# Weight rounding moved from the attention phase to the mixing phase, and couplings interleaved with another step

## The chip, the cores and the metric

One core of one Trainium2 chip runs the whole program. The metric is device microseconds of one execution; the figure before is the median of three runs. PE is TensorE, DVE VectorE, ACT ScalarE, POOL GpSimd, SP SyncE, which only issues DMAs here.

## What is computed

Three layers over 4 batches of 768 tokens and 384 features. The first is a recurrent attention with a delta rule (8 heads of 48), shown here as the reference has it; the second a gated unit with mixing over tokens; the third a channel mix.

```python
for t in range(S):
    y[:, :, t] = einsum('bhd,bhde->bhe', q[:, :, t], state)
    v_old = einsum('bhde,bhd->bhe', state, kt)
    state = state + bt * einsum('bhd,bhe->bhde', kt, vt - v_old)
...
h = gelu(x @ w_in); u, v = halves(h); v_n = layernorm(v) * g_ln
x = x + (u * (einsum('ts,bsd->btd', w_sg, v_n) + b_sg)) @ w_out
...
k = relu(xk @ w_k); out = sigmoid(xr @ w_r) * (k * k @ w_v)
```

xk and xr are blends of x with x one token earlier.

## The kernel before, in words

**Attention phase (to about 326 us).** Tokens are cut into 12 blocks of 64 (s = 0 to 11); two blocks make a group g (0 to 5); the 32 pairs of batch and head of a block are worked in two octets o = 0, 1 of 8 rows of 2. For each group, `gram` (L321) makes products of keys on PE, `solver` (L359) inverts the 32x32 diagonal blocks on DVE, many small instructions that end in a transpose to DT (L456), and `couple(g, k)` (L465) makes, for each half k = 0, 1 of the group, the off-diagonal block: 32 PE matmuls (L472; 64 records each, since a fp32 matmul appears twice) and two ACT copies back into GL (L475). For each s and o five steps follow: `st_rq` (L494: products with the state, residual r on DVE), `st_d` (L533: 32 matmuls of 32x32 with DT, then an ACT copy u1), `st_n` (L544: matmuls of GL with u1), `st_s` (L558: state) and `st_y` (L573: outputs, DMA into xT by `store_x`, L595).

The order on PE, ACT, DVE and POOL is the order of emission (a manual schedule). `slots` (L818) gives four slots per s; slot 0 is n(s-1, 1) and rq(s, 0), slot 1 d(s, 0), s(s-1, 1) and y(s-1, 1), slot 2 n(s, 0) and rq(s, 1), slot 3 d(s, 1), s(s, 0) and y(s, 0). `run` (L871) emits a slot's steps in three rounds (matmuls, first copies, rest), then `fill` and three calls of `tick` (L851). A call of `tick` is one point; 24 points are a group.

`fill` (L715) puts matmuls of the second layer's input projection between: v units (L651) of weight 1 and u units (L703) of weight 0.5; a v unit waits until 6 weight jobs are done, a u unit until 12. How many is planned: for points 24 to 95 from PACE, INST and COST (L880), otherwise from a slot time (SLOT, SLOT0) less the costs in `used` (L895). Where there are none, `keep_warm` (L737) runs idle matmuls.

`background` (L744), called in `tick` with a budget of 1.62 us of DVE, takes instructions from three kinds of streams by SHARE: layer-norm steps, the solver, weight jobs. It first runs what is due in `later`: a coupling goes there, two points after the solver's end, aligned to six points, the second half six points on (L459); scale_v four points after a y step (L593).

**Weight jobs.** The matrices w_in, w_out, w_k, w_r, w_v are of 64-bit numbers and are rounded to a high and a low part. `narrow` (L155) does one piece: a load on SP (L161), an ACT scaling (L165), four DVE instructions (L170, L172, L174, L176), a POOL add (L178) and then, `lag` points later, `split` (L118): an ACT copy to the high part and a POOL subtraction to the low part. `scratch` (L194) adds a store to DRAM by SP (L203). In the attention phase run 12 jobs of w_in (lag 0), 8 of w_out and 12 of w_k (128x256 each), in that order; two at a time early, later started every EVERY = 6 points while fewer than RUN run, from point 100 on every second point. `reload` (L209) and L1131 bring the rounded parts back.

**Mixing phase (326 to about 490 us).** Eight halves (b, t). `mix` (L1062) does four steps d of 18 matmuls (L976), with DVE (L1072, L1074, L1078) and ACT (L1075) after each; `project` (L1086) is the output projection of a half, 3 x 12 matmuls (L152) and one DVE add each (L1094). Beside them `side` (L1028) emits DVE instructions of weight jobs, here 3 of w_r and 8 of w_v: SD = 2 at each step d, one at each part of `project`. `turns` counts steps d; at most NRAW = 3 jobs are open. u and v come by SP (L1059, L244). After the seventh half POOL issues the reload of w_k (L1131), after the eighth that of w_v (L1142).

**Last phase.** Blends, `w_k`, `w_v` and `w_r` products (L152) and the output.

## Time and profile before

| | us |
|---|---|
| median of 3 runs | 741.13 (737.92 to 743.28) |
| the profiled execution | 737.01 |
| its span, first to last instruction | 735.2 |
| PE busy | 682.0 (93%) |
| DVE busy | 502.0 (68%) |
| ACT busy | 364.3 (50%) |
| POOL busy | 202.6 (28%) |
| mean granted TensorE clock | 0.972 of full speed |

The page gives one execution. A line such as L152 can be a helper's, so groups are told apart by their tiles. "Issue" in the chain is time in which an engine waited for nothing that the profile shows. In the chain and the waits, the name after an arrow is the instruction that ended last before the waiting one could start. Names of tiles such as sw0l or sg are slots that several tiles share in turn.

### The profile page before, as it was taken

How to read it: one execution, taken by the hardware profiler on the slowest of the kernel's cores; microseconds unless marked ns; L12 is line 12 of the kernel's file. 1: busy time of each engine (PE TensorE's matmuls, PEld its weight loads, DVE VectorE, ACT ScalarE, POOL GpSimd, SP SyncE). 2: the span in 40 equal slices, each digit the busy share in tenths (PEclk: the TensorE clock that was granted, in tenths of full speed). 3: DMA queues.
4: the chain of work that ended last, by engine and by line, in shares of the span. 5: the costliest groups of instructions: out<-in, count | busy, mean ns of one | idle time of the engine just before them, and what ended most of it. 6: DMA issues, size and time to landing. Idle time of an engine off the chain costs nothing.

```text
span 735.2 us, 24465 instructions
## 1 busy us (share of the span) xinstructions
PE 682.0 (93%) x10669; PEld 618.3 (84%) x10669; DVE 502.0 (68%) x992; ACT 364.3 (50%) x696; POOL 202.6 (28%) x257
## 2 busy tenths in 40 slices
PE   2568889999997998899999999999999999999998
PEld 2436668878886897789999999998989898999997
DVE  5999989978979695723558676798655564736251
ACT  2235676777765766864322323156444453525140
POOL 4033543454444555643041615330000000000000
PEclk8678999999998999999999999999999999999999
DMA  8402654665665458548853444367000000000000
GB/s 246 108 30 72 158 141 121 177 177 178 155 200 179 126 178 219 186 132 232 284 185 132 153 148 150 109 200 186 33 12 23 22 21 22 18 27 11 33 12 32
DMA packets 80938, 88.71 MB, mean 121 GB/s; under 512 B 24704, under 2 KB 63616, under 8 KB 80832
## 3 DMA queue, kind: packets, MB, share of 16 engines
q1 hardware_dynamic: 75520, 77.33, 35.6%
q0 software_dynamic: 5312, 9.83, 5.0%
q8 instruction: 83, 1.36, 0.8%
q14 instruction: 23, 0.19, 0.1%
HBM read 56.60 MB, written 25.82 MB: 112 GB/s over the span
## 4 chain that ended last, share of the span: by engine, by line
PE 78%; DVE 10%; issue 4%; ACT 4%; DMA 2%; POOL 1%; SPq 1%; ACTq 0%; POOLq 0%; DVEq 0%
PE ms L152 34%; PE ms L976 12%; PE ms L703 7%; PE ms L651 6%; PE ms L579 3%; PE rk L537 2%; PE rk L550 2%; PE rk L514 2%; PE sps L565 2%; PE ms L742 2%; PE ms L334 2%; DVE sg L356 2%; PE ms L472 2%; PE qk L517 1%; DVE sg L396 1%
## 5 line engine op out<-in xcount | busy, mean ns | idle before, releaser
L152 PE MATMUL ms<-wvh,sl 128*128 128x384 f32 x192 | 64.7, 337 | 0.5 <-DVE sl L124 0.5
L152 PE MATMUL ms<-wvh,sh 128*128 128x384 f32 x192 | 64.6, 337 | 0.1
L152 PE MATMUL ms<-wvl,sh 128*128 128x384 f32 x192 | 64.5, 336 | 0.0
L178 POOL TENSOR_TENSOR na<-na,raw 128x256 int32<-128x256 int32 (+2 forms) x43 | 38.7, 899 | 93.3 <-ACT gh L1075 40.7
L1075 ACT ACTIVATE gh<-w 128x384 fp32r<-128x384 f32 x32 | 16.8, 526 | 93.7 <-DVE w L1074 93.7
L152 PE MATMUL ms<-xm_hi,sw0h 128*128 128x512 f32 x144 | 56.1, 390 | 0.0
L152 PE MATMUL ms<-xm_hi,sw0l 128*128 128x512 f32 x144 | 56.1, 389 | 0.0
L152 PE MATMUL ms<-xm_lo,sw0h 128*128 128x512 f32 x144 | 56.0, 389 | 0.0
L124 DVE TENSOR_TENSOR sl<-sg,sh 128x512 fp32r<-128x512 f32 x48 | 33.2, 691 | 28.8 <-ACT sh L121 28.6
L976 PE MATMUL ms<-sw0h,g 128*128 128x384 f32 x192 | 50.2, 335 | 0.0
L976 PE MATMUL ms<-ws1h,g 128*128 128x384 f32 x192 | 49.9, 334 | 0.0
L121 ACT ACTIVATE sh<-sg 128x512 fp32r<-128x512 f32 x48 | 30.3, 631 | 33.9 <-DVE sg L1188 33.9
L1205 DVE TENSOR_TENSOR sg<-sg,ms 128x384 f32<-128x384 f32 x24 | 13.3, 552 | 49.4 <-PE ms L152 49.4
L356 DVE TENSOR_TENSOR sg<-sg,Yt 128x512 f32<-128x512 f32 (+4 forms) x72 | 43.3, 611 | 1.3
L530 POOL TENSOR_SCALAR_AFFINE_SELECT SQ<-SQ 64x512 f32<-64x512 f32 x36 | 28.2, 783 | 48.6 <-ACT SQ L529 47.5
L1187 ACT ACTIVATE sg<-ms 128x512 f32<-128x512 f32 x48 | 28.6, 596 | 26.1 <-PE ms L152 24.1
L1188 DVE TENSOR_TENSOR sg<-sg 128x512 f32<-128x512 f32 x48 | 33.2, 691 | 10.9 <-ACT sg L1187 10.8
L334 PEld LDWEIGHTS ms<-kT 64*32 64x32 f32 x640 | 18.5, 124 | 22.4 <-issue 14.5
L703 PE MATMUL ms<-xl,wiu_hi 128*128 128x256 f32 x144 | 37.0, 296 | 0.0
L152 PEld LDWEIGHTS ms<-wvh,sl 128*128 128x128 f32 x192 | 36.1, 188 | 0.8 <-DVE sl L124 0.8
L703 PE MATMUL ms<-xh,wiu_lo 128*128 128x256 f32 x144 | 36.4, 291 | 0.0
L152 PEld LDWEIGHTS ms<-wvh,sh 128*128 128x128 f32 x192 | 36.1, 188 | 0.4 <-ACT sh L121 0.4
(244 smaller groups left out, 2151.0 us busy)
## 6 DMA issues: line engine op xcount, KB each, us to landing
u_d<-ug SPq DMA_DIRECT2D x24, 256.0 KB, 4.0
u<-u_d SPq DMA_DIRECT2D x16, 384.0 KB, 4.1
vn_d<-v SPq DMA_DIRECT2D x22, 256.0 KB, 3.5
vk<-in_vk_dram SPq DMA_DIRECT2D x24, 192.0 KB, 4.0
vk<-in_vk_dram SPq DMA_DIRECT2D x12, 384.0 KB, 3.7
st<-vn_d SPq DMA_DIRECT2D x18, 256.0 KB, 3.1
out_dram<-sg SPq DMA_DIRECT2D x24, 192.0 KB, 1.9
kT<-in_kt_d_dram SPq DMA_DIRECT2D x8, 512.0 KB, 5.3
```

Of the source, the lines that this page charges most:

```text
L121: A.activation(hi, src, AF.Copy)
L124: eng_lo.tensor_tensor(lo, src, hi.bitcast(F32), op=ALU.subtract)
L152: T.matmul(pt, lhsT=a, rhs=b, start=(i == 0), stop=(i == n - 1))
L178: G.tensor_tensor(a.bitcast(I32), a.bitcast(I32), w_lo.bitcast(I32), op=ALU.add)
L334: T.matmul(gps[r:r + 32, p, c0:c1], lhsT=t[r:r + 64, u, 0:32], rhs=t[r:r + 64, u, c0:c1], start=True, stop=True)
L356: V.tensor_tensor(tv, vw(a_t, a_off, a_dims), vw(b_t, b_off, b_dims), op=ALU.mult)
L530: G.affine_select(out=pt, in_=pt, pattern=[[0, 8], [1, C]], compare_op=ALU.is_gt, fill=0.0, base=0, channel_multiplier=-1)
L651: T.matmul(vstat[g, b], lhsT=a[:, c], rhs=w[:, c], start=first, stop=last)
L703: T.matmul(vstat["u"][:, 2 * P * d:2 * P * d + 2 * P], lhsT=w[:, c, ds_], rhs=a[:, c].rearrange("p b t -> p (b t)"), start=first, stop=last)
L976: T.matmul(pt[:, :DM], lhsT=v[:, ds_], rhs=w, start=(c == 0 and i == 0), stop=(c == 5 and i == 2))
L1187: A.activation(r, pt, AF.Relu)
L1188: V.tensor_tensor(r, r, r, op=ALU.mult)
```

## The change

- The 12 jobs of w_k leave the attention phase and stand in the mixing phase, in a queue of their own ahead of those of w_r and w_v; each queue has three jobs open. `side` emits one DVE instruction at each step d and five at each part of `project`, and `turns` advances in `project` too.
- In a job the POOL add, the ACT copy and the POOL subtraction are apart: one, two and one points later in the attention phase; in the mixing phase only the copy is a turn later.
- `couple` gives its matmuls and its copies apart. The even d steps d(2g, 0) and d(2g, 1) emit, after each four of their matmuls, four of the coupling's half o; the copies follow in the third round.
- Jobs start every 12 points; three run at once also early; one w_in job more is started at the start; scale_v comes six points after y.
- PACE 0.0157 to 0.0152, SLOT 5.315 to 5.1, PAIR and AHEAD in the plan of `fill`.

```diff
-SV = 60
-RUN = (3, 2, 3)
+RUN = (3, 3, 3)
-EVERY = 6
+EVERY = 12
+NMIX = 12
-JLAG = 2
-SLOT = 5.315
+SLOT = 5.1
-LAGC = 2
-PACE = 0.0157
+PACE = 0.0152
+PAIR = 0.45
+AHEAD = 4.0
-SD = 2
+SD = (1, 5)
...
-        G.tensor_tensor(a.bitcast(I32), a.bitcast(I32), w_lo.bitcast(I32), op=ALU.add)
+        yield hops[0], lambda: G.tensor_tensor(a.bitcast(I32), a.bitcast(I32), w_lo.bitcast(I32), op=ALU.add)
...
-        yield lag, lambda: split(A, G, af, hi, lo)
+        yield 1 + hops[0], lambda: A.activation(hi, af, AF.Copy)
+        yield hops[0], lambda: G.tensor_tensor(lo, af, hi.bitcast(F32), op=ALU.subtract)
...
-    jobs += j1
+    jobs += j1[:-NMIX]
+    wk_jobs = j1[-NMIX:]
     n_rest = len(jobs)
+    hops = [1]
...
-            if g:
-                p = point[0] + LAGC
-                p += -p % 6 if p % 6 > 2 else 0
-                for k in range(2):
-                    later.append((p + 6 * k, lambda k=k: couple(g, k)))
...
             DT, u0, t = DTs[s // 2], (s % 2) * NPR + 8 * o, RQs[o, "r"]
+            w = couple(s // 2, o) if s % 2 == 0 else None
             for p in range(8):
                 for b0 in (64, 96, 0, 32):
                     T.matmul(RQs[o][b0:b0 + 32, p, 0:D], lhsT=DT[b0:b0 + 32, u0 + p, :],
                              rhs=t[b0:b0 + 32, p, :], start=p == 0, stop=True,
                              skip_group_check=True)
+                if w:
+                    for u in (2 * p, 2 * p + 1):
+                        w[0](u)
             yield
             u1 = RQs[o, "u"] = ap2.tile([P, 8, D], F32, name="u1", bufs=1)
             A.activation(u1, RQs[o][:, :, 0:D], AF.Copy)
+            yield
+            if w:
+                w[1]()
...
-                    after(4, lambda: scale_v(s + 2))
+                    after(6, lambda: scale_v(s + 2))
...
-                while len(running) < 2 and len(jobs) > n_rest:
-                    start_job(LJ0 if point[0] else LJ)
+                while len(running) < 3 and len(jobs) > n_rest:
+                    start_job(LJ0 if point[0] else (LJ, LJ, 2 * LJ0)[len(running)])
...
-            used[0] += sum(COST[f.__name__[3:]] for f, _, _ in todo)
+            even = [f for f, s, _ in todo if s % 2 == 0]
+            used[0] += sum(COST[f.__name__[3:]] for f, _, _ in todo) + PAIR * (st_d in even)
...
-                fill(sum(PACE * INST[f.__name__[3:]] - COST[f.__name__[3:]] for f, _, _ in todo)
-                     / (0.235 - 2 * PACE))
+                fill((sum(PACE * INST[f.__name__[3:]] - COST[f.__name__[3:]] for f, _, _ in todo)
+                      + (st_d in even) * (PACE * 128 - PAIR)) / (0.235 - 2 * PACE)
+                     + AHEAD * ((st_rq in even) - (st_d in even)))
...
-    jobs += j2 + j3
-    live, turns, starts, owing = [], [0], [4 + 2 * i for i in range(NRAW)], []
+    hops[0] = 0
+    live, turns, owing = [], [0], []
+    lanes = [(jobs + wk_jobs, [4 + 2 * i for i in range(NRAW)]), (j2 + j3, [7 + 2 * i for i in range(NRAW)])]
...
-        side(SD)
+        side(SD[0])
         turns[0] += 1
...
-            side(1)
+            side(SD[1])
+            turns[0] += 1
```

## Rows read from the trace of the kernel before

**Rows 1.** stretches: us, busy us per engine (x instructions), PE clock, DMA share, GB/s

```profile
42.00:104.00 62.00, 53.28 (x1688) 37.68 (x1688) 57.97 (x132) 37.48 (x80) 29.68 (x38) 0.91 0.37 98
104.00:233.00 129.00, 122.30 (x3721) 104.55 (x3722) 113.66 (x242) 90.49 (x179) 60.83 (x79) 0.99 0.60 170
233.00:326.00 93.00, 86.47 (x2227) 77.16 (x2227) 61.79 (x134) 66.75 (x129) 47.51 (x65) 0.95 0.59 169
326.00:490.00 164.00, 164.00 (x966) 162.46 (x962) 105.54 (x187) 51.19 (x99) 52.43 (x54) 1.00 0.56 177
...
222.00:237.00 15.00, 10.73 (x304) 9.38 (x304) 14.62 (x31) 9.16 (x18) 7.63 (x10) 0.81 0.54 160
```

**Rows 2.** chain of waits, 219 to 240 us: start us, us, what

```profile
224.67 1.49 DVE na L170
...
229.26 0.42 DVE na L176
...
230.85 1.95 DVE sw0l L456
...
232.84 1.92 PE ms L472 x64
```

**Rows 3.** waits of PE, 245 to 330 us: line, releaser, us in total, times, longest

```profile
PE ms L472 <- DVE DT L456: 1.9, 1, 1.9
```

**Rows 4.** chain of waits, 262 to 330 us

```profile
285.73 0.40 ACT raw L121
...
309.71 0.42 ACT raw L121
```

**Rows 5.** chain of waits, whole run

```profile
60.12 2.34 issue
...
86.24 0.99 issue
...
148.03 1.13 PE ms L472 x64
...
152.46 0.81 PE rk L537 x64
153.27 0.85 PE sps L565 x32
154.12 1.08 PE ms L579 x31
155.20 0.94 issue
...
365.44 6.36 PE ms L152 x36
```

**Rows 6.** stretches between issue waits, and one of the steady part

```profile
62.46:73.62 11.16, 10.19 (x382) 8.44 (x383) 11.13 (x22) 7.20 (x16) 3.37 (x5) 0.85 0.19 52
73.62:87.23 13.61, 11.99 (x385) 8.86 (x384) 13.47 (x23) 9.40 (x21) 6.76 (x9) 1.00 0.55 154
138.00:185.00 47.00, 45.32 (x1398) 38.81 (x1392) 39.19 (x92) 33.38 (x67) 22.16 (x31) 1.00 0.61 174
```

**Rows 7.** timeline of PE at 49 us: start us, us, instruction, count

```profile
49.09 0.21 PE L472 MATMUL ms<-sw0l,sg 32*32 32x32 f32 x1
49.10 0.22 PE L537 MATMUL rk<-r,sw0l 32*32 32x48 f32 x4
49.13 0.21 PE L472 MATMUL ms<-sw0l,sg 32*32 32x32 f32 x2
```

**Rows 8.** groups by line and form, ACT: busy us, mean ns, idle before

```profile
L571 ACT ACTIVATE SQ<-sps 48x384 f32<-48x384 f32 x34 | 16.5, 486 | 3.1 <-PE sps L565 2.5
...
L584 ACT ACTIVATE yst<-ms 128x512 f32<-128x512 f32 x24 | 14.3, 594 | 4.6 <-PE ms L579 3.1
...
L475 ACT ACTIVATE GL<-ms 32x512 f32<-32x512 f32 x8 | 4.7, 589 | 1.9 <-PE ms L472 1.8
```

**Rows 9.** waits of SP's queue, 340 to 495 us

```profile
SPq L203 <- POOL raw L124: 51.9, 8, 11.9
```

## The prediction

> **What bounds the kernel now.** I read the stretches first. From 326 us on PE is busy without a hole (164.0 of 164 up to 490 us, and behind that the chain of waits stays on PE's L152), so nothing that the change adds or takes away there can make that part shorter: 735.2 - 326 = 409 us stand, and only a new wait could lengthen them. What can be had lies before: 62 us hold 8.7 us of idle PE from 42 to 104, 129 hold 6.7, and 93 hold 6.5 [rows 1]. Then the chain of waits says who holds PE there. Three kinds:

> One is DVE's solver, late for the coupling. From 222 to 237 us PE is busy for 10.7 of 15 us at a mean granted clock of 0.81, so part of it at the lower of the two levels: 4.3 us idle, and about 0.19 x 10.7 = 2.0 us of slower running, 6.3 us together [rows 1]. The chain through it is DVE without a break, and inside the solver's last products stand four instructions of a weight job (L170, L172, L174, L176): 1.49 + 0.42 + 0.21 + 0.42 = 2.54 us; then the transpose of 1.95 us, and at its end the coupling (L472) [rows 2] (of the four the first and the last). The jobs run in the order w_in, w_out, w_k; this is the 24th of 32, so one of w_k.

> The second is the end of attention, from 278 us: the last group's first coupling waits 1.9 us for the same transpose (DT, L456) [rows 3], and behind it the chain runs through ACT, where seven pieces belong to w_k jobs (0.40, 0.24, 0.43, 0.31, 0.44, 0.97 and 0.42, the one of 0.97 on POOL), 3.2 us [rows 4] (of the seven the first and the last).

> The third is "issue", PE waiting for nothing that the profile shows. Between the ends of the waits near 60, 72 and 86 us PE takes 382 + 383 = 765 instructions in 11.16 us (14.6 ns each), then 385 + 384 = 769 in 13.61 us (17.7 ns each) [rows 5, 6]. They come back after nearly equal numbers of instructions, not after equal work, and grow where short instructions stand close. From 138 to 185 us, where long matmuls are filled in between, it is 2790 instructions in 47 us, 16.8 ns each, and the wait is down to single ones of 0.94 us [rows 5, 6].

> **The change part by part.** The sum is made against the profiled execution: 737.0 us, a span of 735.2 and 1.8 around it. The median of the three runs is 741.1, 4.1 above; I add that at the end.

> Coupling beside d. Twelve halves of 64 PE matmul records (32 calls) leave their own places, where one takes 1.13 us; a d takes 0.81 [rows 5]. Put together they cost 1.94 if nothing overlaps (gain 0), 1.13 if d vanishes beside the coupling (gain 0.81). The nearest row is the one place where the two already touch, at 49.1 us: the first coupling matmul stands between the d's, and groups of d and of coupling alternate within 80 ns, each with a duration of 0.20 to 0.22 [rows 7]. So different 32x32 places of the array work at once although they share rows. The coupling uses two places and d four; I take 1.30 for the pair, near the overlapped end, where the row is: gain 0.64. It counts only where PE is what is late. I count seven halves (the second of group 1, and groups 2 to 4); in group 0 and the first of group 1 the issue waits rule, in group 5 ACT. 7 x 0.64 = -4.5 us; ends 0 and -9.7 (12 x 0.81).

> [...]

> Pacing. The plan per group of 24 points is worked out from the constants. Before: rq 0.96, d 1.21, n 0.20, s 0.16, y -0.10 four times each, plus 0.88 for four grams and two halves, 15.0 us over 0.2036 = 74 units of fill. After: 2.21 four times, 0.82 four times and 1.50 twice, 15.1 over 0.2046, also 74. In the late slots 8 x 5.315 less 21.2 of work against 8 x 5.1 less 19.3 are 21.3 and 21.5 us. As much fill is placed, closer together by what the coupling gives back. Cost 0 by itself; AHEAD only shifts 4 units (about 1 us) from behind an even d to before it.

> Solver at 222 us. With w_k gone and a w_out job every 12 points instead of a weight job every 6, half of the jobs of that group go, and the coupling no longer comes up behind the solver's end but in a fixed slot, somewhat later. The four instructions cost 2.54, the coupling was 3.1 late. I take -5.0 of the 6.3; ends 0 and -6.3. Next late is rq's residual on DVE, which has room: DVE has 113.7 of 129 us busy before and loses five to six jobs of 1.3 to 2.5 us.

> End of attention. All w_k pieces go there; the eight w_out jobs, started at points 24 to about 102, are past. -1.9 for the wait and about -2.1 of the 3.2, because ACT also carries the splits of w_sg and v: -4.0; ends 0 and -5.1.

> New wait: n for the coupling's copies. They now stand behind u (as wide as a copy of s), two copies of s (0.49) and y (0.59) on ACT, two of 0.59 [rows 8]. y's matmuls end 1.9 us after d's, its copy at 2.5, the coupling's at 3.7. PE reaches n after 1.9 us and the slot's fill: 8.9 units or 2.1 us when paced, 5.1 - 3.2 = 1.9 in the late slots, so at 3.8 to 4.0. It just fits; with one more ACT instruction of 0.6 ahead n waits half a microsecond, and behind n the next rq stands on PE. Only the first half of each group matters (six): +1.5; ends 0 and 7.1 (6 x 1.18).

> Issue. An even d with its coupling, s and y is 384 PE instructions in 1.30 + 1.93 = 3.2 us, where d, s and y were 256 in 2.7. Groups 1 to 3 go from 16.8 towards 16.4 ns per instruction, still slower than 14.6. +1.0; ends 0 and 11.3 (12 waits of 0.94).

> Hops and the third early job. A job's POOL add, ACT copy and POOL subtraction come one point later each, four points per job. That unblocks ACT and POOL but holds the last w_in job, for which u units wait, some 5 us longer. The same fill is done later: 0; ends -1 and +4.

> w_k in the mixing phase. 12 jobs of four DVE instructions, at most 2.54 us each, are 30 us where DVE is idle for 164.0 - 105.5 = 58.5 [rows 1]. They are hidden behind PE, mostly beside the projection: 15 of them at 0.42 are 6.3 us beside 6.36 of PE [rows 2, 5]. On ACT, POOL and SP each adds two, two and two (SP's are its load, L161, and its store, L203, which leave SP's queue in attention: 24 DMAs, counted with the gains there); SP has waited 51.9 us for POOL in its stores (L203) already [rows 9], and behind these stores stand the loads of u and v, issued a half ahead. w_k's stores must land before its reload after the seventh half, which w_k's priority sees to. +0.5; ends 0 and +6. If the cover went, v's loads would hold ACT's split, with it gh, and with it PE.

> Sum: -4.5 - 5.0 - 4.0 + 1.5 + 1.0 + 0 + 0.5 = -10.5, so 726.5 profiled and 730.6 as a median.

> **Rivals.** (a) The solver stays late: jobs started at points 72 and 84 stand in the same place, and PE comes earlier. Against it: half as many. The solver term is -1: 734.6. (b) No overlap, d and coupling in turn: 735.1. (c) ACT takes over: n waits in full for the copies (7.1 instead of 1.5) and of the last stage only the 1.9 is saved: -10.5 + 5.6 + 2.1 = -2.8, 738.3. For it: ACT is 67 of 93 us busy at the end. (d) Slower: the issue wait. At 14.6 ns 384 instructions need 5.6 us and get 3.2, 2.4 short; 256 in 2.7 were 1.0 short. If PE has no reserve for the 1.4 in between, some 100 instructions, it pays at all twelve, +16.8 instead of +1.0: +5.3, 746.4. For it: the 2.34 us at 60 us, in the densest place. Against it: the steady groups take the 1.0 nearly always without a wait.

> [...]

> **How the numbers follow.** Forecast 0.50, (a) 0.15, (b) 0.10, (c) 0.13, (d) 0.12. The time is the forecast's, 730.5. Its own ends reach from about 720 (all overlaps, all stalls gone) to 738; (d) lies above 743 and is left out. So 720 to 743. One per cent, 7.4 us, is about what a measurement here can tell from no change: faster means below 733.7, slower above 748.5. That is 0.44 of the forecast's 0.50, (a) 0.06, (b) 0.04, (c) 0.01, whose centres lie just above the bound: faster 0.55. Slower: 0.05 of (d) and 0.05 of mishaps in the mixing phase, 0.10. The same 0.35.

> **What would show it.** Right: attention ends some 10 us earlier and the rest stays at 409; the chain has no L170 to L176 before the solver's transpose of group 4; d with coupling takes 1.2 to 1.4 us; ACT shows no w_k pieces after 270. Wrong: pairs of 1.9; an n that waits for ACT's L475 copies; issue waits after each even d; or holes in PE between 326 and 517, under a load of v or a store of w_k.

## The result and the profile after

The changed kernel takes 746.2 us (median of 16 runs, 740.5 to 750.6) against 739.3 for the kernel before: a ratio of 1.0095 with a 95% interval of 1.0072 to 1.0118, slower by about 1%. The forecast was 730.5.

| profiled execution | before | after | change |
|---|---|---|---|
| whole | 737.0 | 744.6 | +7.6 |
| attention, to the first mix matmul | 326.5 | 322.3 | -4.2 (forecast -11.0) |
| mixing, to the first matmul of the last phase | 167.8 | 180.1 | +12.3 (forecast +0.5) |
| last phase | 240.8 | 240.4 | -0.4 |
| PE busy, DVE busy | 682.0, 502.0 | 678.1, 503.9 | |

The same stretches as in [rows 1], of the kernel after:

```profile
42.00:104.00 62.00, 49.49 (x1688) 35.79 (x1690) 59.94 (x140) 34.48 (x72) 28.23 (x34) 0.92 0.33 91
104.00:233.00 129.00, 123.94 (x3750) 106.53 (x3735) 104.18 (x215) 89.89 (x170) 52.45 (x67) 0.97 0.54 151
233.00:326.00 93.00, 85.00 (x2245) 75.72 (x2245) 50.46 (x110) 64.45 (x118) 36.97 (x57) 0.98 0.53 141
326.00:490.00 164.00, 155.39 (x886) 152.45 (x885) 118.11 (x221) 57.09 (x116) 64.98 (x71) 0.98 0.62 205
222.00:237.00 15.00, 14.66 (x450) 12.61 (x449) 13.67 (x34) 9.99 (x20) 7.09 (x8) 1.00 0.56 162
```

The line from 222 us is the one with the solver's stall before: PE was busy for 10.73 of 15 us at a clock of 0.81 (1.00 up to 231.3 us, 0.50 from there to 237), now for 14.66 at 1.00. From the last d of group 3 to the first of group 4 (block 8) it is 16.5 us before (222.0 to 238.5) and 10.2 after (222.8 to 233.0). But the line from 326 us, which had no hole before, is busy for 155.39 of 164. Who holds PE there is one line of PE's waits from 326 to 505 us:

```profile
PE ms L986 <- ACT g L121: 8.0, 2, 6.0
```

Three timelines show the longer of the two. (Line numbers have moved: L986 is the mix matmul, L1084 and L1086 are w, L1087 is gh, L1090 gl, L182 a job's ACT copy, L121 the ACT half of a split.) PE (start us, us, instruction, count, idle before and what ended it):

```profile
414.39 0.34 PE L986 MATMUL ms<-sw0h,g 128*128 128x384 f32 x1
420.76 0.69 PE L986 MATMUL ms<-sw0h,g 128*128 128x384 f32 x1 [6.03 <-ACT g L121]
421.25 0.52 PE L986 MATMUL ms<-sw0l,g 128*128 128x384 f32 x1
421.87 1.01 PE L986 MATMUL ms<-sw0h,g 128*128 128x384 f32 x2
...
425.85 0.34 PE L152 MATMUL ms<-gh,wo_hi 128*128 128x384 f32 x1
```

DVE's timeline, same columns:

```profile
408.29 0.82 DVE L172 TENSOR_SCALAR na<-na 128x256 f32<-128x256 f32 x1
...
416.50 1.23 DVE L176 SCALAR_TENSOR_TENSOR na<-raw,na 128x384 uint32<-128x384 uint32 x1
417.65 0.60 DVE L1084 SCALAR_TENSOR_TENSOR w<-ms,g_sb,b_sb 128x384 f32<-128x384 f32 x1
418.29 0.93 DVE L1086 TENSOR_TENSOR w<-w,u 128x384 f32<-128x384 f32 x1
419.15 1.22 DVE L1090 TENSOR_TENSOR gl<-w,gh 128x384 fp32r<-128x384 f32 x2
```

ACT's:

```profile
419.26 0.52 ACT L1087 ACTIVATE gh<-w 128x384 fp32r<-128x384 f32 x1 [3.26 <-DVE w L1086]
419.69 0.51 ACT L182 ACTIVATE raw<-na 128x384 fp32r<-128x384 f32 x1
420.10 1.13 ACT L121 ACTIVATE g<-st 128x512 fp32r<-128x512 f32 x2
```

The same w on DVE and the same split on ACT in the kernel before:

```profile
413.84 0.60 DVE L1072 SCALAR_TENSOR_TENSOR w<-ms,g_sb,b_sb 128x384 f32<-128x384 f32 x1
415.50 1.66 ACT L121 ACTIVATE g<-st 128x512 fp32r<-128x512 f32 x3
```

PE is done with the last step d of the half at 408 us. Its w starts at 417.65, because fourteen DVE instructions of the jobs, emitted up to five behind each of the three products of the projection, stand ahead of it (the first and the last are shown; they take 0.28 to 1.23 us each). ACT gets gh only then, and behind gh, in its fixed order, stand a job's copy and the split of v's last chunks. The fourth chunk of the next mix, to which PE comes when the third ends (its last matmul starts at 414.39), needs that split. The loads of v that the split reads were issued from 405.1 to 408.0 us and landed 3.6 to 3.8 us later, so v's load was not what was late. Behind the hole, until 425 us, a matmul takes 0.52 us instead of 0.34: the granted clock is 0.50 from 420.8 to 425.2 us; the clock records of this execution and of that of the kernel before have 0.50 and 1.00 and no other value. A second hole, of 2.0 us, stands at 461 us; the matmuls behind that one take 0.34 us, and the clock is 1.00 from 463 to 470 us.

In attention a pair with nothing in its way does what was forecast of it. PE's timeline of one; L539 is d, L471 the coupling, L573 the next step:

```profile
149.29 0.24 PE L539 MATMUL rk<-r,sw0l 32*32 32x48 f32 x4
149.32 0.22 PE L471 MATMUL ms<-sw0l,GL 32*32 32x32 f32 x2
...
150.40 0.27 PE L471 MATMUL ms<-sw0l,GL 32*32 32x32 f32 x6
150.60 0.24 PE L573 MATMUL sps<-sw0h,vk 64*48 64x48 f32 x1
```

From 149.29 to 150.60 it takes 1.31 us (1.30 forecast; 1.94 in turn, as the sum of the two alone). But only two of the eight pairs of groups 1 to 4 are so short; from the first d to the first s they take 1.31 to 1.93 us, 12.9 together. Twelve pairs of 1.31 would be 7.6 us shorter than 1.94 each, the solver's stall is gone, and yet the first mix comes only 4.2 us earlier. Among PE's waits from 42 to 322 us stand three that were not there, or smaller, before:

```profile
PE rk L539 <- DVE r L492: 5.8, 2, 4.8
...
PE ms L587 <- ACT v L668: 3.4, 1, 3.4
PE ms L587 <- issue: 3.1, 2, 1.6
```

d waits for rq's residual (4.8 us of it ahead of the d at 90.8 us), y for ACT and for nothing that the profile shows.

From d to d the loss has one place. In groups 1 to 4 the four stretches from the last d of a group to the first of the next sum to 49.8 us before and 37.5 after: there stood the solver's stalls and the first half of the coupling. Those from a group's second d to its third, which hold the second interleaved pair with its s and y, sum to 49.4 and 60.2. The other two kinds have 90.0 and 87.9. Of the 10.8 us that are lost, 2.9 are the coupling that came there (the four pairs take 6.1 us, where a d takes 0.81), 4.9 are three waits for nothing that the profile shows (1.5 and 1.6 at y, 1.8 at a gram), and the rest is slow running behind the one at the gram, near 202 us:

```profile
PE ms L339 <- issue: 1.8, 1, 1.8
203.50:210.40 6.90, 6.90 (x107) 5.73 (x108) 2.36 (x4) 3.36 (x7) 0.86 (x2) 0.51 0.14 38
```

(The first line is of PE's waits from 181.7 to 276.4 us, the second a stretch as above: the clock granted is 0.51.)

### The profile page after: what moved, and what is told of

Read it like the earlier page. It is cut to its first block, busy times and chain, and to the rows that moved or that the text cites. A ratio compares the mean times of both kernels' runs of the same rounds, so it can differ in the third digit from the quotient of the medians.

```text
span 742.8 us, 24474 instructions
## 1 busy us (share of the span) xinstructions
PE 678.1 (91%) x10666; PEld 615.2 (83%) x10666; DVE 503.9 (68%) x992; ACT 369.1 (50%) x696; POOL 202.3 (27%) x257
## 4 chain that ended last, share of the span: by engine, by line
PE 49%; DVE 7%; issue 3%; DMA 3%; ACT 2%; POOL 2%; SPq 0%; POOLq 0%; ACTq 0%; DVEq 0%
PE ms L152 34%; PE ms L986 5%; PE ms L711 3%; PE ms L659 3%; DVE w L1084 1%; DVE w L1086 1%; DMA xT<-yst 1%; PE ms L587 1%; DVE na L170 1%; POOL raw L183 1%; DMA st<-vn_d 1%; DVE na L174 1%; DVE gl L1090 1%; DVE na L176 1%; DVE na L172 1%
## 5 line engine op out<-in xcount | busy, mean ns | idle before, releaser
L152 PE MATMUL ms<-wvh,sl 128*128 128x384 f32 x192 | 64.7, 337 | 0.0
L152 PE MATMUL ms<-wvl,sh 128*128 128x384 f32 x192 | 64.6, 337 | 0.0
L152 PE MATMUL ms<-wvh,sh 128*128 128x384 f32 x192 | 64.6, 336 | 0.0
L986 PE MATMUL ms<-sw0h,g 128*128 128x384 f32 x192 | 52.5, 346 | 8.6 <-ACT g L121 8.0
L152 PE MATMUL ms<-xm_hi,sw0h 128*128 128x512 f32 x144 | 56.3, 391 | 0.4 <-ACT xm_hi L121 0.4
L152 PE MATMUL ms<-xm_lo,sw0h 128*128 128x512 f32 x144 | 56.2, 390 | 0.2 <-DVE xm_lo L124 0.2
L152 PE MATMUL ms<-xm_hi,sw0l 128*128 128x512 f32 x144 | 56.1, 390 | 0.0
L986 PE MATMUL ms<-ws1h,g 128*128 128x384 f32 x192 | 49.9, 335 | 0.0
L1219 DVE TENSOR_TENSOR sg<-sg,ms 128x384 f32<-128x384 f32 x24 | 13.3, 554 | 50.5 <-PE ms L152 50.5
L986 PEld LDWEIGHTS ms<-sw0h,g 128*128 128x128 f32 x192 | 35.7, 193 | 10.1 <-ACT g L121 8.7
L121 ACT ACTIVATE sh<-sg 128x512 fp32r<-128x512 f32 x48 | 30.1, 630 | 28.2 <-DVE sg L1202 28.2
L182 ACT ACTIVATE raw<-na 128x256 fp32r<-128x256 f32 (+2 forms) x31 | 13.6, 437 | 57.6 <-POOL na L178 57.5
L1087 ACT ACTIVATE gh<-w 128x384 fp32r<-128x384 f32 x32 | 16.8, 525 | 49.9 <-DVE w L1086 49.9
L337 PEld LDWEIGHTS ms<-kT 64*32 64x32 f32 x640 | 19.3, 128 | 24.7 <-issue 17.1
L339 PE MATMUL ms<-kT 64*32 64x64 f32 (+1 forms) x640 | 22.2, 231 | 17.7 <-issue 17.5
L346 ACT ACTIVATE sg<-ms 128x256 f32<-128x256 f32 x32 | 17.6, 578 | 38.5 <-PE ms L339 38.4
```

The lines of the kernel that those rows point to most:

```text
L121: A.activation(hi, src, AF.Copy)
L152: T.matmul(pt, lhsT=a, rhs=b, start=(i == 0), stop=(i == n - 1))
L339: T.matmul(gps[r + 32:r + 64, p, c0:c1], lhsT=t[r:r + 64, u, 32:64], rhs=vw2(t, r, 64, u * C + 32 - c0, [(-32, (c1 - c0) // 32), (1, 32)]) ...
L986: T.matmul(pt[:, :DM], lhsT=v[:, ds_], rhs=w, start=(c == 0 and i == 0), stop=(c == 5 and i == 2))
```

## The experiments

Times are medians with the ratio to the kernel before that ran beside them; experiments are compared with each other by these ratios, times 740 us. In the family of i_later the lines are a few further on (L153 for L152, L994 for L986).

### The hole in the mixing phase

**m_cs3**: three chunks of the next mix ahead of the projection instead of four.

```diff
-CS = (5, 4)
+CS = (5, 3)
```

> The changed kernel, but the next batch's mixing is begun ahead of the projection with three chunks of v instead of four. Theory (the DVE steps of jobs beside the projection in the middle of a t = 1 half hold up the last step's w, behind it ACT's copy gh and behind that the split of v's chunks 3 to 5): PE no longer meets chunk 3 there, but the projection that it takes instead needs gh and gl of the same late step d = 3, ready at about 420.5 us where PE arrives some 1.6 us after 412.7. So the hole at 414 us shrinks from 6.4 to some 5 us, but does not go: 743 to 746 us as a median (746 for the change). Rival (v's load from DRAM is late because SP's stores stand before it): the chunk is met 6.4 us later, the hole goes, and the time falls by about 8 to 11 us, to 735 to 738.

Measured: 737.8 us, 0.9956 (0.9928 to 0.9984), so 10.3 us less than the change, and a little faster than the kernel before: the rival's number. But DVE and ACT run the same instructions in the same order as above, with w at 418.62, gh at 420.25 and v's split from 421.09. So the chain from the jobs' steps to the split stands; PE only meets it in another place. PE's timeline of m_cs3:

```profile
418.40 0.33 PE L986 MATMUL ms<-sw0h,g 128*128 128x384 f32 x1
418.57 0.34 PE L152 MATMUL ms<-gh,wo_hi 128*128 128x384 f32 x1
...
419.63 0.33 PE L152 MATMUL ms<-gh,wo_hi 128*128 128x384 f32 x1
420.74 0.44 PE L152 MATMUL ms<-gl,wo_hi 128*128 128x384 f32 x1 [0.78 <-DVE gl L1090]
```

PE now goes through seven products of the projection (1.2 us) and waits for gl of the third column, which stands behind w on DVE and is there at 420.7, 1.0 us ahead of v's first split. And w stands 92.4 us behind the first mix here (418.62 - 326.3), 95.4 in the change (417.65 - 322.3), since the half before lost less too. Together 5.2 us: the 6.0 us of idle PE become 0.8.

**l_cs4** puts the fourth chunk back into i_later (below), a kernel with another attention.

> i_later with four chunks of the next mix ahead of the projection, as the kernels before and after have it. Theory (v's split stands on ACT behind the last w's gh, and that behind the jobs' steps on DVE, whatever attention does): the holes of 6 us and 2 us and the slower matmuls behind them come back, +6 to +10 on i_later: 738 to 742, with the first mix still near 315 us. Rival (the holes belong to the interleaved attention): 731 to 735.

Measured: 739.7, 0.9968 (0.9940 to 0.9997); +6.5 us on i_later, the first mix at 316.2. The waits of PE from 326 to 500 us are those of the change, a little smaller:

```profile
PE ms L994 <- ACT g L122: 6.8, 2, 4.8
PE ms L994 <- DVE g L125: 0.5, 1, 0.5
```

So the hole belongs to the mixing phase and costs 6.5 to 10.3 us, whatever attention does. The profiles say the same of the phase alone: from the first mix to the last phase 180.1 us in the change and 170.0 in m_cs3, 181.5 in l_cs4 and 172.7 in i_later, 10.1 and 8.8 us apart.

**m_late25**, **m_sd22**, **m_pd1**: other places for the same steps.

```diff
-SD = (1, 5)
+SD = (2, 5)              # m_late25, and side(SD[1] if t else 1) in project
+SD = (2, 2)              # m_sd22
...
-PD = 2
+PD = 1                   # m_pd1
```

> The changed kernel, with the same weight jobs in the mixing phase at other places: two DVE instructions at each step d, one at each part of the projection that stands in the middle of a t = 1 half, five at each part of the one that follows a whole batch. Theory (place, not amount): the two holes at 414 and 460 us (6.4 and 2.3 to 3.1 us) and the low clock behind the first (about 2 us) go, no hole over 1 us in the phase; about 734 to 737 us as a median, faster than the kernel before (739). Rival (DVE, POOL and SP simply have too much beside PE, wherever it stands): holes of the same sum elsewhere, 744 to 748. Second rival (SP's stores hold the loads of v): holes at 414 and 460 stay, since the number of stores is the same.

> The changed kernel with two DVE instructions of jobs at each step d and two at each part of any projection, in place of one and five. Theory: six instead of fifteen stand before the last step's w, 9 x 0.55 = 5 us less, so the hole at 414 us falls from 6.4 to under 1.5 us and the clock stays up: 736 to 739 us; but more jobs of w_v are left for the end of the phase, where they may hold the blends by 1 to 2 us. Rival (amount): 744 to 748.

> The changed kernel (four chunks ahead) with the projection of the half before put behind the second mix of a half instead of the third, so that the steps of the weight jobs beside the projection stand on DVE ahead of the third mix's w and one whole mix (3.1 us of PE) more lies between them and the place where PE needs v's third chunk. Theory (those steps, ahead of the last w and with it of gh and of v's split, make the holes at 414 and 461 us): both holes under 2 us, total 736 to 740. Rival (the holes come from the loads or from the sum of DVE's work in the phase): holes of 4 us or more remain, 743 to 748.

Measured: 748.1 (1.0101, 1.0065 to 1.0137), 755.1 (1.0188, 1.0147 to 1.0228) and 753.0 (1.0169, 1.0110 to 1.0227). Each moved the wait. m_late25 has no hole at 414 us, but PE stands for gl near 405 and 407 (1.3 and 1.9 us idle), for 0.7 and 1.3 at 425 and 464, and for 2.7 at the end; m_sd22 gets through too few steps, and the rest stands ahead of the last phase, 13.7 us at 505; in m_pd1 the hole at 421 is 0.7 and the one at 460 is 3.4, but the projection, one mix earlier, waits three times 1.0 us for gl. All three missed what I expected. In m_pd1 the slack that I gave to v's split was taken from gl. m_late25 lies at the number of its rival, that the amount is too much wherever it stands; against that rival stands m_cs3, which has the same steps in the same order and is 10.3 us shorter. (m_sd22's profile is of its slowest execution, 763.7 us.)

**l_46**, **l_47**: i_later with fewer steps ahead of the last w and more at the other projection.

```diff
-            side(SD[1])
+            side(6 if t else 4)      # l_47: 7 if t else 4
```

> i_later with four steps of the jobs behind each product of the projection that stands ahead of a half's last w, and six behind each product of the other projection, instead of five at both. Theory (each of those steps moves w, gh and gl of the last column by 0.5 to 0.6 us, and PE waits 1.3 to 1.4 us for them at 410 and 449 us): both waits under 0.4 us, 729 to 731. Rival (the steps that are left end later and hold the last phase, or w's other places): 732 to 736.

> i_later with four steps of the jobs behind each product of the projection that stands ahead of a half's last w, and seven behind each of the other. In l_46 (four and six) the waits at 410 and 449 us were gone, but steps were left at the end and held the last phase by 5.2 us. Theory (one more step at the other projection, where nothing waits for DVE, takes these up): no wait over 1.5 us at the end of the phase, 727 to 731. Rival (steps beside the other projection delay the next w as well): 732 to 736.

Measured: 733.6 (0.9906, 0.9875 to 0.9937) and 731.4 (0.9878, 0.9844 to 0.9912), against 0.9880 for i_later. In both the two waits ahead of the last w are gone, as the theory has it. In l_46 the steps that are left hold the last phase:

```profile
PE ms L153 <- ACT xm_hi L122: 4.8, 1, 4.8
```

In l_47 that is 2.3 us. So the steps ahead of the last w cost the 2.1 us that PE waits for gl in i_later, and moved elsewhere they cost as much again at the end of the phase.

### Attention: the place of the coupling

**a_attn**: the change with w_k's jobs back in attention (EVERY, RUN and the jobs' pace as before).

> The changed kernel with w_k back in the attention phase (a job every 6 points, two at a time) and the mixing phase as before; the interleaved couplings, the hops, the third early job and the fill's plan stay. The trace of the change has attention 4.2 us shorter and the rest 11.8 longer. If the couplings and the plan bring the gain in attention, this is 3 to 5 us faster than the kernel before: 734 to 736. If the gain comes from w_k's absence, it is as before or slower, 739 to 742, with DVE's L170 to L176 again ahead of the transpose of group 4. In both cases no hole between 330 and 490 us.

Measured: 750.3, 1.0123 (1.0083 to 1.0164), the first mix at 334.8 us, 8 us later than before (and 5.4 us of waiting at the end of the mixing phase, where steps are left). With w_k in its old place the rest of the change makes attention longer, by this one execution.

**i_turn**, **i_later**: m_cs3 with the coupling in turn behind d in the same slot, and m_cs3 with the coupling in places of its own and the old pacing.

```diff
-                if w:
-                    for u in (2 * p, 2 * p + 1):
-                        w[0](u)
+            if w:                    # i_turn: behind the loop over p
+                for u in range(16):
+                    w[0](u)
...
+                for k in range(2):   # i_later: at the solver's end, as before
+                    later.append((p + 6 * k, lambda k=k: whole_couple(g, k)))
```

> The changed kernel with three chunks of the next mix ahead of the projection instead of four (as in m_cs3, 737.8 us), and the 16 products of a half of the coupling issued behind d's matmuls instead of between them: same instructions, same slot, same copies, no interleaving. Theory (attention is paid by waits for instructions and the clock behind the dense blocks, so what the interleaving saves in a pair is given back at once): a pair takes 1.94 us instead of 1.31 but the waits shrink, total 737 to 740. Rival (the overlap's 12 x 0.63 us, or the seven that I counted, is real on the path): 742 to 746.

> m_cs3 with the halves of the coupling in places of their own between the stages and with the pacing of the kernel before (slot 5.315, pace 0.0157), w_k still rounded in the mixing phase. Theory (the interleaving gives back what it saves): 734 to 739, the first mix at 322 to 327, waits for issue in attention back to some 11 us. Rival (the interleaving is what brought m_cs3 below the kernel before): 741 to 746, first mix 331 or later.

Measured: i_turn 740.5 (0.9998, 0.9969 to 1.0026), i_later 731.7 (0.9880, 0.9831 to 0.9928; four runs). In the even d's slot the overlap is worth 3.1 us by the medians (the two intervals overlap, so the size is rough), so it is not given back whole. A clean pair in turn takes 1.76 us in i_turn, not 1.94, and the eight of groups 1 to 4 take 15.2 us, 12.5 in m_cs3. But the slot costs 8.7 us against places of the coupling's own, where every pair is in turn. The stretch from the first d of group 3 to the first d of group 5 shows it, the same work in each, columns as in [rows 1]. Before:

```profile
187.10:282.40 95.30, 88.98 (x2542) 78.49 (x2541) 80.49 (x180) 63.27 (x123) 47.93 (x62) 0.96 0.62 175
```

After:

```profile
181.70:276.40 94.70, 90.37 (x2557) 78.84 (x2556) 75.09 (x172) 63.43 (x120) 41.13 (x56) 0.96 0.52 147
```

m_cs3:

```profile
185.60:280.20 94.60, 89.49 (x2561) 78.09 (x2562) 74.67 (x172) 63.70 (x120) 43.12 (x56) 0.96 0.54 148
```

i_later:

```profile
183.10:271.60 88.50, 87.13 (x2542) 76.74 (x2541) 73.62 (x170) 61.49 (x119) 41.73 (x54) 1.00 0.58 157
```

Before, 6.3 us are idle, most of them the solver's two stalls (3.1 and 1.9). After and in m_cs3 that stall is gone and the pairs are shorter, but 4.3 and 5.1 us are idle and the clock stands at 0.96: only 0.6 and 0.7 us are gained. In i_later 1.4 us are idle at a clock of 1.00: 6.8 us are gained. What the idle time of m_cs3 is shows its chain of waits:

```profile
246.05 0.85 PE sps L573 x32
246.90 0.20 PE ms L587
247.10 2.76 issue
249.86 1.97 PE ms L587 x31
251.84 3.29 PE ms L659 x7
```

One matmul of y, then 2.76 us for nothing the profile shows, then the other 31 in 1.97 us, and seven v matmuls in 3.29 us, 0.47 each. In the kernel before, nine take 2.07, 0.23 each, at about the same time:

```profile
247.38 2.07 PE ms L651 x9
```

Behind the wait the granted clock is 0.50 (249.8 to 252 us) and 0.55 (to 256), and that costs nearly as much again: 3.29 - 7 x 0.23 = 1.7 us, and 0.9 in y. The same wait stands behind the first matmul of the same y in the change's profile, with 1.57 us; there the clock stays at 1.00 (248.6 to 256 us), and the seven v matmuls take 1.82 us.

**i_pace**, **i_own**: place and pacing apart. i_pace is m_cs3 with the old SLOT, PACE and no AHEAD; i_own is i_later with the new SLOT and PACE.

> m_cs3 (the halves of the coupling interleaved with the even d's, three chunks ahead of the projection) with the pacing of the kernel before: slot 5.315 instead of 5.1, pace 0.0157 instead of 0.0152, no units shifted ahead. Theory (what costs in attention is the place: 384 short instructions in one block and a clock that falls behind the wait): 735 to 741, as m_cs3 with 737.8. Rival (the tighter pacing is what costs, not the place): 730 to 734, as i_later with 731.7.

> i_later (halves of the coupling in places of their own, w_k in the mixing phase) with the pacing of the changed kernel, slot 5.1 and pace 0.0152. Theory (place): 730 to 735, as i_later. Rival (pacing): 736 to 741.

Measured: 742.3 (1.0011, 0.9987 to 1.0036) and 732.6 (0.9888, 0.9855 to 0.9922). The place decides, by 5 us at the new pacing and 10 at the old.

**i_spread**: m_cs3 with seven units of the fill set between d, s and y.

> m_cs3 with the fill of each slot that has an even d split: four units directly behind d with its coupling, three behind s, the rest at the end, so that the 384 short instructions of d, s and y no longer stand in one block; the sum of the work in a slot is the same. Theory (waits for instructions follow the density of short instructions): issue waits in y behind the second even d go from 17 us in all to under 10, total 731 to 736. Rival (the waits stand at fixed places in the program or come from ACT and DVE): 736 to 741.

Measured: 752.0, 1.0142 (1.0083 to 1.0200). The issue waits fell as the theory said (the rows from 104 to 315 us sum to 6.9 us, 12.9 in m_cs3), but the fill puts every step of the slot back, and n waits for ACT's copies of the coupling:

```profile
PE rk L558 <- ACT GL L476: 2.9, 4, 1.5
...
PE rk L558 <- ACT sg L476: 2.3, 4, 1.5
...
PE rk L558 <- ACT sw0h L476: 1.9, 4, 0.8
```

These three lines are 7.1 us; m_cs3 has 0.8 in the same.

**l_dense**: i_later with the coupling directly behind rq, ahead of the fill: n, rq and coupling are one block of 320 short instructions. **l_first**: the coupling one slot later, ahead of d: 384 in a block, with the copies first on ACT.

```diff
+            due = [e for e in tight if e[0] <= point[0] + 2]
+            for e in due:            # l_dense: behind the slot's matmuls
+                tight.remove(e)      # l_first: ahead of them, at p + 3
+                e[1]()
```

> i_later with each half of the coupling issued directly behind rq's matmuls, ahead of the slot's fill instead of behind it: n, rq and coupling are then one block of 320 short instructions, where 192 and 128 stood with some eight long fill matmuls between them. The coupling's copies are ready earlier, not later; everything else and the sum of the fill stay. Theory (density: waits for instructions and the lower clock behind them are the price of a block longer than 256): 735 to 741, issue waits in attention up from 12.8 us by 4 or more, first mix at 320 or later. Rival (what cost in the even d's slot was the later copies and the order on ACT, not density): 730 to 733.

> l_dense with each half of the coupling issued ahead of d in the even d's slot instead of behind rq one slot earlier: the slot is again one block of 384 short instructions (coupling, d, s, y) as in i_turn, but the coupling's copies now stand first on ACT. Theory (instructions come at some 15 to 17 ns each, and 384 with some nine fill matmuls in a slot of 5.3 us ask for 13.5): 736 to 743, issue waits from 104 to 315 us at 8 us or more, where l_dense has 4.5. Rival (the late copies of i_turn and of the change were the price): 727 to 732, issue waits under 6 us.

Measured: l_dense 728.3 (0.9842, 0.9812 to 0.9872; four runs), l_first 736.1 (0.9971, 0.9944 to 0.9997). l_dense took my theory down in its first form: a block of 320 is not dear; if anything it is 3 us better than 192 and 128 apart. l_first showed that the late copies are not the price either: with the copies first, the even d's slot costs 9.5 us again. The same stretch of groups 3 and 4, first of l_dense:

```profile
186.00:273.40 87.40, 86.87 (x2545) 76.50 (x2545) 75.52 (x171) 60.99 (x117) 39.87 (x54) 1.00 0.58 158
```

And of l_first, from the coupling ahead of the same d's:

```profile
184.90:277.20 92.30, 88.16 (x2552) 77.36 (x2551) 73.41 (x172) 62.27 (x119) 41.08 (x54) 1.00 0.54 150
```

Half a microsecond idle against 4.1. Issue rows of PE's waits from 104 to 315 us sum to 4.5 us in l_dense and 9.1 in l_first, as before (4.5) and after (8.2), m_cs3 (12.9) and i_turn (14.4). By these profiles half of the 9.5 us are such waits; the last group gives most of the others (from its first d to the first mix 42.0 us in l_dense, 46.9 in l_first), where PE also waits for ACT's copies of v and u units. Over all kept profiles the sum of these rows is 8.2 to 15.0 us in the nine kernels with the coupling in the even d's slot, and 1.9 to 8.4 in the nine with places of its own (6.9 in i_spread, with fill between).

Where these waits stand, the profiles do settle. Count PE's instructions in the order in which they start (matmuls, weight loads and the few of its sequencer): every wait of over 0.3 us for nothing that the profile shows, from 40 to 335 us in all nineteen profiles, 229 of them, has a count ahead of it that is 193 to 195 above a whole multiple of 256; none stands anywhere else. About one such place in five has a wait. The rows leave out the sequencer's instructions and so show it within a few. In the kernel before, from the end of the wait near 86 us to that of the next two ([rows 6] has the two stretches ahead of these), then in the change, from the wait at the gram near 202 us to the one at y near 248:

```profile
87.23:91.75 4.52, 3.40 (x127) 2.49 (x127) 3.82 (x7) 1.65 (x4) 3.47 (x5) 1.00 0.79 177
91.75:103.87 12.12, 10.56 (x383) 7.80 (x384) 9.85 (x30) 9.80 (x20) 6.38 (x10) 1.00 0.45 108
202.54:248.62 46.08, 44.05 (x1277) 38.10 (x1276) 33.82 (x80) 27.88 (x54) 16.39 (x24) 0.93 0.46 128
```

That is 254, 767 and 2553, one, three and ten times 256. It is also why m_cs3 and the change wait behind the same matmul of the same y.

### What w_k's leaving is worth

**l_attn**: i_later with w_k's jobs back in attention; hops and early jobs as changed.

> i_later with w_k's jobs back in attention (a job every 6 points, two running) and the mixing phase's jobs paced as in the kernel before; hops apart and three early jobs are kept. Theory (w_k's leaving is what shortens attention, by DVE's and ACT's time): first mix at 323 to 329, mixing phase 146 to 149 us, total 736 to 742. Rival (the hops and the third early job did it): first mix at 314 to 319, total 727 to 733.

Measured: 743.7, 1.0048 (1.0013 to 1.0082), the first mix at 325.9 us (315.5 in i_later, 326.5 before). So 10.4 us of attention are w_k's; hops and the third early job give nothing. (The mixing phase ends there in a wait of 5.4 us, since with this pace steps are left, and is 1.1 us longer than in i_later.) Groups 3 and 4 take 95.2 us, like the kernel before; the end, from the first d of group 5, takes 43.9 us with w_k and without.

**l_best**: l_dense with four and seven steps beside the projections.

> l_dense with four and seven steps of the jobs behind the products of the projections, as l_47. Theory (the two waits of 0.8 and 1.7 us ahead of the last w go, the end of the phase gives 2 us back): 726 to 730. Rival (it costs what it gives): 728 to 732.

Measured: 729.0 (0.9885, 0.9853 to 0.9917): no better than l_dense. l_dense is the version to keep, 1.6% faster than the kernel before and 2.5% faster than the change.

## Why the prediction was wrong

Two steps failed, one of them in its sign; most of the sum stood.

*w_k in the mixing phase, +0.5 (0 to +6): measured +12.3 in the profiled execution, and 6.5 to 10.3 by undoing the hole alone.* This is the first failed step. I set 30 us of instructions against 58.5 us in which DVE is idle, and fifteen of them against the projection's 6.36 us. Sums of a phase do not say who stands behind. On DVE the steps stand ahead of the last w of the half, on ACT gh ahead of v's split. They are also longer than I took them: the fourteen take 8.3 us together, 0.59 each and not 0.42. I named the last link ("v's loads would hold ACT's split, with it gh, and with it PE") with the order turned round: the loads were there, and gh held the split. What w had to spare was in the profile before, and I had not looked it up: how long before PE needed the split DVE came to w. In the kernel before w stands 87.4 us behind the first mix and the split 89.0 (415.50 - 326.47), after 95.4 and 97.8. PE comes to the fourth chunk 92.3 us behind the first mix in both. So the split's first piece (0.63 us) had been done 2.6 us ahead of PE, it comes 8.8 us later, and 6.2 us are missing: the hole of 6.0. Without the hole the phase takes 170.0 us in m_cs3 and 172.7 in i_later where it took 167.8, so 2.2 to 4.9 us are left, within the ends of the term.

*Coupling beside d, -4.5: the size of a clean pair was right (1.31), the place was not priced.* In its slot the overlap gives 3.1 us (i_turn), since most pairs are not clean and in turn they take less than 1.94, and the slot takes 8.7: a net of +5.6 where -4.5 stood. This is the second failed step, with *Issue, +1.0*, the term that should have carried it: in the stretch from 104 to 315 us issue alone is +3.7 in the change's profile and +8.4 in that of m_cs3, which has the same attention, and the lower clock behind some of these waits (0.51 from 203.5 to 210.4 us in the change's profile), which I had priced at nothing, is on top.

*Pacing, 0*: right (i_pace, i_own: within 1 us with places of their own; 4.1 us worse at the old pacing in the even d's slot, where the new one is thus right).

*Solver at 222 us, -5.0*: right, about 4.5. From the d ahead of the stall to the d behind it the change is 6.3 us shorter; some 1.8 of that is the coupling, which no longer stands there (the same stretches ahead of groups 2 and 3, where nothing stalled for long, are 1.7 and 1.9 shorter). From l_attn to i_later, with the coupling in places of its own in both, the stretch falls from 14.4 to 10.1. But rq's residual, which was to have room, now holds d for 5.8 us. It costs little: from the last d of group 0 to the first of group 1, where 4.8 of it stand, 12.5 us instead of 11.6.

*End of attention, -4.0*: only the wait for the transpose was found. From the last d of group 4 to the first of group 5 it is 11.3 us before and 8.9 after, 13.6 in l_attn and 9.3 in i_later. In its place the coupling waits 1.6 us for nothing that the profile shows, and behind that first d nothing is gained: 44.1 us before, 45.9 after, 43.9 in l_attn and in i_later.

*n waits for the coupling's copies, +1.5*: right; PE's waits of n for ACT sum to 1.5 us in the change's profile from 42 to 322 us.

*Hops and the third early job, 0*: right (l_attn).

Of the rivals, (d), the issue wait after each even d, has the measured time, 746.4, and half of the cause. It is not the whole: its 16.8 us were all in attention, where the runs give 8.7 and 9.5 with the clock (i_turn, l_first), and the other half of the loss is in a phase that it does not touch. (b) fell with the pair's 1.31, (a) with the 222 us line. (c) shows in one place: y waits 3.4 us for ACT's v ahead of 295 us; n, for which it was priced, waits 1.5 and not 7.1.

What stays open: why the places 256 apart have long waits where 384 short instructions stand in a block, and no more than the kernel before where 320 do (l_dense). Their rate does not settle it. From the n at 238.88 us to y at 246.83 m_cs3 issues 548 instructions in 7.95 us, 14.5 ns each, and waits; l_dense has 532 in 7.07 us, 13.3 each, from 236.95 to 244.02, and does not. Also, attention of one and the same code ended at 322.3, 326.3, 326.4, 328.7 and 332.8 us in the profiles of the change, m_cs3, m_late25, m_pd1 and m_sd22, so a single execution does not size these waits; the medians above do.

## What to carry to other kernels

Before work is put into an engine's idle time, look up the instruction behind it in that engine's order, when it is needed and by whom; the idle sum of a phase is not slack. When two groups of instructions overlap, the overlap's gain is read from the pair, but its price from the slot: how long the block of short instructions has become and what stands behind it (here 384 in the even d's slot cost 8.7 us in i_turn and 9.5 in l_first; 320 behind rq cost nothing in l_dense). A shorter step that ends in a wait can lose twice, by the wait and by the clock behind it (2.76 and 2.6 us in m_cs3 at 247 us). And a gain is credited to a stall only from the step ahead of it to the step behind it: a time counted from the start of the run carries all that was won and lost before.
